# Loading keys and receptances eight tokens to a partition in a linear-attention and hypermixer kernel

## The chip, the cores and the metric

The kernel runs on one core of one Trainium2 chip. The metric is the device time of one execution in microseconds. Before the change it is 106.31 us, the median of three runs (105.37 to 106.67).

## The reference

Four batches, eight heads, 768 tokens, 48 values per head. For each head a 48 x 48 state runs over the tokens:

```
cur   = (u * k_t) outer v_t
y_t   = r_t @ (state + cur)
state = w_t[:, None] * state + k_t outer v_t
```

The rows y of all heads, 384 wide, are x of the second part:

```
W_tok = (x @ w_q) @ (x @ w_k)^T / 8          (768 x 768 in each batch)
out   = relu(W_tok @ x) @ w_out
```

All inputs and the output are float32. W_tok is not built: the kernel forms T = (x w_k)^T x, which is 64 x 384, and multiplies by x w_q.

## The kernel before, in words

**Units.** The work is cut into 12 units of 256 tokens (3 to a batch), each of two chunks of 128 tokens. For a unit W, K, R and V are loaded from DRAM. `load` (L291) puts the tokens 2p and 2p+1 of the unit into partition p, so a load is one transfer of 384 KB with 128 x 8 pieces of 384 bytes. Each of the four tensors has a ring of four buffers. V of the last batch is loaded in another way: `WHOLE = (3,)`, `load_whole` (L296), four transfers for the whole batch in 192-byte pieces that are already in the token order which the chunks need.

**A unit's steps**, by the keys that the plan gives them: `ln` (ScalarE, log of the decay, L453), `k16` and `r16` (casts to bf16, L463, mostly GpSimd), `cw` (16 matmuls of the log decay with the mask CM: a running sum over the tokens of a chunk), `ep` and `en` (ScalarE, exp of that sum and of its negative, L491 and L496), `kT` and `rT` (8 transposes each on TensorE), `ks` (copy out of PSUM), `qT` (L522), `RT` = rT x ep (VectorE, L531), `KT` = ks x en (GpSimd or VectorE, L539), `A` (products of KT and RT, chunk by chunk), `AM` (the same under the mask US, L608), `kb` and `kd` (KT transposed back), `sn` and `SB` (the state), `yi` and `ya` (the output rows), `X` (L712), which also adds `Vd`, V times the u term (GpSimd, L588). V comes into chunk order with `v16` (cast, GpSimd, L556) and `vp` (4 matmuls with the permutation PM); `VB` copies it out of PSUM. In the last batch `VB` is one cast on GpSimd (L550).

Within a chunk, column j*64 + p stands for token 2p + j: even tokens first, then odd ones. The masks CM and US and the vectors gx and gv are made for that order. RT needs ep of the token before; ep is therefore written with a shift (66 columns on for j = 0, 1 on for j = 1) into blocks of 132 columns whose first is 1.

**A batch's second part**: `xt`, `XT`, `wk`, `wq`, `QK`, `T`, `TS`, then per unit `mx` (3 matmuls), `rl` (ReLU, L396 on ScalarE or L398 on VectorE), `fp` (matmuls with w_out), `os` (copy), `st` (store).

**The order** is written out by hand: every step has a rank in `RANK`, and `ALT` says which engine takes those steps that several can do. Each engine's queue is its steps sorted by rank. `Plan.order` (L80) plays the queues through with estimated durations, only to give PSUM banks and to merge the queues into one order of program text. All loads and nearly all stores are issued from SyncE in one queue, so a transfer that waits for a buffer, or a store that waits for its `os`, holds what stands behind it. `WARM` matmuls with zeros are placed among TensorE's early steps, 9 more stand at its start.

All matmuls and transposes have line 240 in the profile (the helper `mm`), all copies L384 or L390 (the helper `copy`).

Of the kernel before, what the change touches and what calls it, by code (L numbers as in the profile page):

```python
# [10 lines left out]
F32 = mybir.dt.float32  # L11
# [22 lines left out]
class Plan:  # L34
# [131 lines left out]
    0, 0, 0, 0, 0, 20, 0, 0, 21, 1, 3, 1, 0, 0, 2, 0, 0, 3, 0, 0, 6, 0, 0, 1, 1, 2, 3, 3, 2, 4, 6,  # L166
    6, 9, 3, 6, 4, 2, 5, 7, 5, 20, 10, 24, 12, 8, 10, 15, 8, 19, 11, 16, 9, 17, 11, 25, 12, 28,
    14, 30, 32, 35, 31, 18, 57, 30, 75, 38, 4, 0, 0, 5, 0, 0, 8, 0, 0, 7, 0, 0, 5, 4, 7, 14, 7, 8,
    18, 27, 9, 15, 16, 10, 6, 23, 14, 34, 17, 12, 38, 20, 41, 22, 26, 13, 33, 17, 36, 19, 42, 45,
    43, 46, 24, 64, 33, 77, 39, 9, 0, 0, 10, 0, 0, 13, 0, 0, 15, 0, 0, 13, 9, 20, 29, 15, 16, 37,  # L170
    44, 19, 25, 23, 13, 14, 47, 24, 51, 27, 20, 49, 26, 54, 29, 48, 25, 52, 27, 58, 68, 61, 65,
    35, 74, 37, 78, 40, 81, 43, 86, 44, 91, 47, 47, 0, 0, 88, 45, 97, 50, 51, 0, 0, 111, 56, 120,
    60, 54, 0, 0, 12, 0, 0, 11, 0, 0, 17, 0, 0, 16, 0, 0, 18, 11, 16, 40, 23, 22, 39, 56, 21, 31,
    30, 15, 17, 55, 29, 63, 34, 22, 60, 32, 67, 36, 53, 28, 66, 34, 71, 38, 70, 72, 73, 80, 41,
    89, 46, 101, 55, 14, 0, 0, 18, 0, 0, 21, 0, 0, 24, 0, 0, 21, 18, 35, 50, 28, 26, 59, 76, 31,
    40, 39, 33, 24, 84, 43, 82, 42, 28, 98, 53, 83, 44, 69, 36, 90, 47, 95, 52, 103, 104, 106,
    105, 57, 119, 63, 136, 68, 22, 0, 0, 19, 0, 0, 23, 0, 0, 27, 0, 0, 37, 19, 23, 79, 42, 41, 62,
    85, 32, 45, 46, 26, 27, 94, 49, 96, 51, 30, 102, 56, 93, 50, 92, 49, 100, 54, 108, 113, 115,
    112, 61, 129, 66, 139, 71, 145, 75, 153, 77, 160, 81, 50, 0, 0, 162, 82, 189, 97, 53, 0, 0,
    173, 88, 190, 98, 52, 0, 0, 26, 0, 0, 25, 0, 0, 30, 0, 0, 32, 0, 0, 48, 25, 31, 99, 53, 52,  # L180
    87, 110, 48, 60, 59, 32, 33, 116, 58, 122, 63, 40, 117, 62, 121, 64, 114, 57, 124, 65, 128,
    68, 132, 135, 133, 134, 72, 141, 74, 172, 87, 28, 0, 0, 29, 0, 0, 36, 0, 0, 33, 0, 0, 51, 29,
    37, 107, 54, 55, 109, 126, 58, 67, 69, 36, 35, 123, 62, 138, 69, 42, 137, 73, 144, 76, 125,
    66, 131, 71, 147, 77, 149, 150, 152, 151, 79, 164, 85, 180, 91, 35, 0, 0, 31, 0, 0, 37, 0, 0,
    34, 0, 0, 61, 34, 38, 127, 65, 64, 118, 130, 59, 70, 75, 41, 39, 143, 73, 140, 70, 47, 157,
    82, 146, 78, 142, 72, 155, 81, 166, 168, 169, 170, 88, 177, 92, 192, 101, 203, 103, 212, 105,
    218, 113, 55, 0, 0, 214, 106, 227, 111, 56, 0, 0, 222, 109, 230, 113, 57, 0, 0, 39, 0, 0, 41,
    0, 0, 38, 0, 0, 45, 0, 0, 46, 0, 0, 67, 43, 44, 148, 78, 76, 154, 158, 80, 84, 85, 48, 51,
    167, 84, 52, 176, 91, 165, 87, 163, 83, 175, 90, 179, 92, 182, 185, 184, 183, 95, 200, 102,
    211, 109, 42, 0, 0, 43, 0, 0, 40, 0, 0, 74, 46, 45, 156, 80, 79, 159, 161, 83, 86, 89, 49, 53,  # L190
    171, 86, 55, 191, 100, 181, 94, 178, 93, 187, 96, 194, 101, 197, 202, 198, 199, 104, 210, 104,
    215, 110, 48, 0, 0, 44, 0, 0, 49, 0, 0, 90, 50, 54, 186, 93, 94, 95, 96, 174, 188, 89, 99, 97,
    56, 98, 58, 57, 193, 100, 59, 60, 196, 102, 206, 105, 195, 99, 201, 103, 205, 208, 204, 207,
    209, 213, 106, 216, 108, 219, 221, 108, 112, 107, 217, 107, 220, 223, 111, 110, 224, 226, 225,
    114, 228, 115, 117, 231, 233, 114, 118, 58, 0, 0, 61, 0, 0, 229, 112, 116, 234, 235, 116, 117,
    59, 0, 0, 60, 0, 0, 232, 115, 118, 236, 237, 119, 119, 120, 62, 0, 0, 1, 2, 4, 5, 7, 8, 10,
    11, 12, 13, 21, 22,
]
ALT = "DDDPDAAAAAAPPDDAADAAPAAPAAADADAAAAAAPPDPAADADPAADADADAPPAPADDAAAAAAAAAPPDPAAADAPPDPAADAAPPAPAAAAAAADAAAAPPDPAAADPPDPADADPPAPPAADADADADDDAAADAAADDA"

WARM = 12
# [3 lines left out]
def kernel(  # L205
# [27 lines left out]
    WHOLE = (3,)  # L233
# [18 lines left out]
    EW = 132  # L252
# [33 lines left out]
    pos1 = const([C, 1], I32, "pos1")  # L286
# [9 lines left out]
    def load_whole(b, q, tl):  # L296
        n_ = H // 2 * NCH
        for j in range(2):
            nc.sync.dma_start(
                out=view(tl, q * n_ * D, [[D, n_], [1, D]], p0=64 * j, pn=64),  # L300
                in_=dataclasses.replace(v, offset=(b * H * S + j) * D + q * n_ * C * D,
                                        ap=[[D2, 64], [C * D, n_], [1, D]]))

    def setup():
# [9 lines left out]
        for j in range(2):  # L314
            nc.gpsimd.iota(pos0[ds(64 * j, 64), :], pattern=[[0, 1]], base=j,
                           channel_multiplier=2)
            nc.gpsimd.iota(pos1[ds(64 * j, 64), :], pattern=[[0, 1]], base=j + 1,
                           channel_multiplier=2)
        nc.scalar.activation(gx, pos0, ACT.Exp, bias=0.0, scale=MU)
        nc.scalar.activation(gv, pos1, ACT.Exp, bias=0.0, scale=-MU)  # L320
        nc.vector.memset(CM, 1.0)
        for c in range(2):
            for j in range(2):
                m = view(CM, j * C, [[64, 2], [1, 64]], p0=c * 64, pn=64)
                nc.gpsimd.affine_select(m, m, pattern=[[1, 2], [2, 64]], compare_op=ALU.is_ge,
                                        fill=0.0, base=-j, channel_multiplier=-2)
        nc.vector.memset(ID16, 0.0)
        nc.gpsimd.affine_select(ID16, ID16, pattern=[[1, C]], compare_op=ALU.not_equal, fill=1.0,
# [5 lines left out]
        nc.vector.memset(US, 1.0)  # L334
        for j in range(2):
            m = view(US, 0, [[64, 2], [1, 64]], p0=j * 64, pn=64)
            nc.gpsimd.affine_select(m, m, pattern=[[1, 2], [2, 64]], compare_op=ALU.is_gt,
                                    fill=0.0, base=-j, channel_multiplier=-2)
# [4 lines left out]
        nc.vector.tensor_scalar_mul(US, US, gv)  # L343
# [5 lines left out]
    def permute():  # L349
        for c in range(2):  # L350
            for j in range(2):
                m = PM[ds(c * 64, 64), ds(j * C + j * 64, 64)]
                nc.gpsimd.affine_select(m, m, pattern=[[1, 64]], compare_op=ALU.not_equal,
                                        fill=1.0, base=0, channel_multiplier=-1)
# [74 lines left out]
    def unit(n, batch):  # L429
# [9 lines left out]
        for name, ap in (("wg", w), ("kg", k), ("rg", r)) + (() if whole else (("vg", v),)):  # L439
            g[name] = ring(name)  # L440
            g[name + "L"] = plan.dma((name, n), 570, 1190 + 250 * (n == 0 and name == 'kg') + 250 * (n > 2),
                                     lambda e, ap=ap, x=g[name].tile: load(b, i, x, ap),
                                     buf=g[name])[1]
# [12 lines left out]
        ln = add(("ln", n), {"A": 846}, f_ln, [g["wgL"]], lw, [g["wg"]])  # L456

        def cast16(name, src, engs):
            o = ring(name)

            def f(e):
                op = dict(A=nc.scalar.copy, D=nc.vector.tensor_copy, P=nc.gpsimd.tensor_copy)[e]
                op(view(o.tile, 0, [[64, H], [512, 2], [1, D]]),  # L463
                   view(g[src].tile, 0, [[D2, H], [D, 2], [1, D]]))
            return o, add((name, n), engs, f, [g[src + "L"]], o, [g[src]])
# [21 lines left out]
        for cs in fine:  # L487
            w_ = 512 * len(cs)

            def f_ep(e, cs=cs, w_=w_):  # L490
                nc.scalar.activation(  # L491
                    view(ep.tile, cs[0] * NP * EW + 66, [[EW, NP * len(cs)], [-65, 2], [1, 64]]),
                    at(cw)[:, ds(cs[0] * 512, w_)], ACT.Exp, bias=0.0, scale=1.0)

            def f_en(e, cs=cs, w_=w_):
                nc.scalar.activation(en.tile[:, ds(cs[0] * 512, w_)],  # L496
                                     at(cw)[:, ds(cs[0] * 512, w_)], ACT.Exp, bias=0.0,
                                     scale=-1.0)
            x = add(("ep", n, cs[0]), {"A": 190 + int(w_ * 0.837)}, f_ep, [cws], ep, [cw])
            y = add(("en", n, cs[0]), {"A": 172 + int(w_ * 0.835)}, f_en, [cws], en, [cw])  # L500
# [3 lines left out]
        def transposed(name, src, step):  # L504
            x = bank()

            def f(e):
                o = at(x, BF16)
                for hp in range(NP):
                    for j in range(2):  # L510
                        mm(view(o, hp * C + j * 64, [[512, 2], [1, 64]]),
                           src.tile[:, ds(j * 512 + hp * 128, 128)], ID16, trans=True)
# [14 lines left out]
        for cs in fine:  # L527
            n4 = NP * len(cs)

            def f_RT(e, cs=cs, n4=n4):  # L530
                nc.vector.tensor_tensor(  # L531
                    view(RT.tile, cs[0] * 512, [[C, n4], [64, 2], [1, 64]]),
                    view(at(rT, BF16), cs[0] * 512, [[C, n4], [64, 2], [1, 64]]),
                    view(ep.tile, cs[0] * NP * EW, [[EW, n4], [66, 2], [1, 64]]), ALU.mult)

# [346 lines left out]
```

## Time and profile before

| | |
|---|---|
| median of three runs | 106.31 us |
| the profiled execution | 106.1 us |
| its span | 104.4 us |
| TensorE busy | 93.2 us (89%), 1651 matmuls |
| VectorE busy | 84.4 us (81%) |
| ScalarE busy | 80.6 us (77%) |
| GpSimd busy | 69.3 us (66%) |
| moved by DMA | 24.65 MB, 236 GB/s over the span |
| chain that ended last | PE 74%, DMA 6%, POOL 5%, DVE 5% |

Read it with the queues in mind: an engine takes its instructions strictly in order, so it is not enough that an operand is there early; the instruction ahead must have gone too. The DMA line of the page counts all 16 DMA engines together: 1.0 is all sixteen at work all the time, and packets that overlap on one engine can bring it above 1. The span holds what the engines do; the time of an execution is 1.7 us longer.

### The profile page before, as it was taken

The page shows a single profiled execution, that of the slowest core. Times are in us where ns is not written, and L with a number is a line of the kernel's source. Part 1 is how long each engine was busy: PE and PEld are TensorE (multiplying, and loading weights), DVE is VectorE, ACT ScalarE, POOL GpSimd, SP SyncE. Part 2 cuts the span into 40 slices and gives each one's busy share as a digit, 9 for nine tenths or more (in the row PEclk, how much of TensorE's full clock was granted, in tenths as well). Part 3 has the DMA queues.
Part 4 walks back from the last instruction along what each step waited for, and adds up shares of the span by engine and source line. Part 5 has one row for each costly group of instructions (what it writes and reads, how often), then busy time and mean ns, then how long its engine had stood idle before and what let it go on. Part 6 is the DMA issues. An engine that isn't in the chain of part 4 may idle for free.

```text
span 104.4 us, 3964 instructions
## 1 busy us (share of the span) xinstructions
PE 93.2 (89%) x1651; PEld 69.4 (66%) x1652; DVE 84.4 (81%) x140; ACT 80.6 (77%) x122; POOL 69.3 (66%) x80
## 2 busy tenths in 40 slices
PE   5999899766998999999999899999999998999910
PEld 2356488544777786767886776887888596866500
DVE  6669996995789979979999889999899699695320
ACT  6348988759879869999999886899897954855830
POOL 6607666979998828959995699999975973000000
PEclk9999999999589999999999999999999999999999
DMA  1999999999999988999999799999993056004791
GB/s 26 296 324 325 325 318 234 309 290 237 301 342 295 246 228 206 303 254 243 310 294 256 195 264 276 244 179 172 292 349 137 0 220 238 0 9 181 295 359 72
DMA packets 56803, 24.65 MB, mean 236 GB/s; under 512 B 54480, under 2 KB 55632, under 8 KB 56784
## 3 DMA queue, kind: packets, MB, share of 16 engines
q1 hardware_dynamic: 56224, 24.19, 84.3%
q8 instruction: 13, 0.21, 0.8%
q10 hardware_dynamic: 560, 0.20, 0.7%
q14 instruction: 6, 0.05, 0.1%
HBM read 19.66 MB, written 4.72 MB: 234 GB/s over the span
## 4 chain that ended last, share of the span: by engine, by line
PE 74%; DMA 6%; POOL 5%; DVE 5%; issue 3%; ACT 2%; SPq 1%; POOLq 0%; DVEq 0%
PE PS L240 74%; DMA vg<-in_v_dram 6%; DVE KT L539 2%; POOL KT L539 2%; POOL v L556 2%; POOL Vd L588 1%; ACT ep L491 1%; ACT MX L396 1%; DVE RT L531 1%; DVE AM L608 1%; SPq L292 1%; DVE qT L522 1%; ACT os L384 0%; DVE Z L306 0%; POOL r L463 0%
## 5 line engine op out<-in xcount | busy, mean ns | idle before, releaser
L608 DVE TENSOR_TENSOR AM<-PS,US 128x1024 bf16<-128x1024 f32 x24 | 29.3, 1219 | 3.4 <-PE PS L240 3.2
L539 POOL TENSOR_TENSOR KT<-ks,en 128x1024 bf16<-128x1024 bf16 (+1 forms) x11 | 20.5, 1864 | 3.6 <-DVE ks L390 3.4
L588 POOL TENSOR_TENSOR Vd<-VB,dd 128x768 bf16<-128x768 bf16 (+1 forms) x14 | 18.1, 1294 | 1.3 <-ACT dd L384 1.2
L712 DVE SCALAR_TENSOR_TENSOR X<-PS,gx,Vd 128x768 bf16<-128x768 f32 (+1 forms) x13 | 12.4, 952 | 2.8 <-POOL Vd L588 1.4
L240 PEld LDWEIGHTS <-KT 48*128 48x128 bf16 (+1 forms) x272 | 10.9, 97 | 5.2 <-issue 2.4
L496 ACT ACTIVATE en<-PS 128x1024 bf16<-128x1024 f32 (+1 forms) x14 | 12.6, 898 | 2.0 <-PE PS L240 2.0
L491 ACT ACTIVATE ep<-PS 128x1024 bf16<-128x1024 f32 (+1 forms) x14 | 12.7, 919 | 1.3 <-ACT XT L384 0.6
L453 ACT ACTIVATE lw<-wg 128x768 bf16<-128x768 f32 x12 | 10.2, 848 | 4.5 <-DMA wg<-in_w_dram 4.4
L240 PE MATMUL PS<-wo,MX 128*128 128x384 bf16 x72 | 13.3, 326 | 0.0
L463 POOL CAST k<-kg 128x768 bf16<-128x768 f32 x11 | 9.0, 825 | 3.3 <-DMA kg<-in_k_dram 3.3
L384 ACT COPY os<-PS 128x768 f32<-128x768 f32 (+1 forms) x13 | 8.6, 680 | 2.5 <-PE PS L240 2.2
L463 POOL CAST r<-rg 128x768 bf16<-128x768 f32 x9 | 7.5, 835 | 4.3 <-DMA rg<-in_r_dram 2.3
L556 POOL CAST v<-vg 128x768 bf16<-128x768 f32 x9 | 7.4, 825 | 3.6 <-DMA vg<-in_v_dram 3.6
L240 PE MATMUL PS<-RT,KT 48*128 48x128 bf16 x192 | 9.7, 221 | 0.0
L240 PEld LDWEIGHTS <-MX 128*128 128x128 bf16 x72 | 6.5, 98 | 4.1 <-issue 0.3
L531 DVE TENSOR_TENSOR RT<-PS,ep 128x1024 bf16<-128x1024 bf16 (+1 forms) x14 | 8.4, 607 | 0.8 <-PE PS L240 0.5
L396 ACT ACTIVATE MX<-PS 128x768 bf16<-128x768 f32 (+1 forms) x11 | 8.2, 755 | 0.7 <-PE PS L240 0.6
L522 DVE TENSOR_TENSOR qT<-PS,ks 128x1024 bf16<-128x1024 bf16 x12 | 8.2, 681 | 0.4 <-issue 0.4
L240 PE MATMUL PS<-Z 128*128 128x512 bf16 x20 | 7.4, 511 | 1.2 <-DVE uT L309 1.2
L384 ACT COPY XT<-PS 128x768 bf16<-128x768 bf16 (+1 forms) x9 | 6.9, 765 | 2.0 <-PE PS L240 2.0
L240 PE MATMUL PS<-ID,r 128*128 128x128 bf16 x96 | 7.7, 226 | 0.4 <-POOL r L463 0.3
L240 PE MATMUL PS<-VB,AM 128*128 128x48 bf16 x192 | 7.9, 184 | 0.1
(83 smaller groups left out, 201.1 us busy)
## 6 DMA issues: line engine op xcount, KB each, us to landing
wg<-in_w_dram SPq DMA_DIRECT2D x12, 384.0 KB, 5.4
kg<-in_k_dram SPq DMA_DIRECT2D x12, 384.0 KB, 5.9
rg<-in_r_dram SPq DMA_DIRECT2D x12, 384.0 KB, 5.9
vg<-in_v_dram SPq DMA_DIRECT2D x9, 384.0 KB, 5.8
out_dram<-os SPq DMA_DIRECT2D x9, 384.0 KB, 3.0
vw<-in_v_dram SPq DMA_DIRECT2D x4, 288.0 KB, 6.2
out_dram<-os SPq DMA_DIRECT2D x5, 192.0 KB, 2.7
wof<-in_moe_w_out_dram SPq DMA_DIRECT2D x1, 576.0 KB, 5.4
```

The source lines that it names most:

```text
L240: return nc.tensor.matmul(o, l, rr, start=start, stop=stop, skip_group_check=True, is_transpose=trans)
L384: nc.scalar.copy(o, i)
L453: nc.scalar.activation(view(lw.tile, 0, [[64, H], [512, 2], [1, D]]), view(g["wg"].tile, 0, [[D2, H], [D, 2], [1, D]]), ACT.Ln, bias=0.0, ...
L463: op(view(o.tile, 0, [[64, H], [512, 2], [1, D]]), view(g[src].tile, 0, [[D2, H], [D, 2], [1, D]]))
L491: nc.scalar.activation(view(ep.tile, cs[0] * NP * EW + 66, [[EW, NP * len(cs)], [-65, 2], [1, 64]]), at(cw)[:, ds(cs[0] * 512, w_)], ACT.E ...
L496: nc.scalar.activation(en.tile[:, ds(cs[0] * 512, w_)], at(cw)[:, ds(cs[0] * 512, w_)], ACT.Exp, bias=0.0, scale=-1.0)
L531: nc.vector.tensor_tensor(view(RT.tile, cs[0] * 512, [[C, n4], [64, 2], [1, 64]]), view(at(rT, BF16), cs[0] * 512, [[C, n4], [64, 2], [1, ...
L539: x.tensor_tensor(KT.tile[:, cols], ks.tile[:, cols], en.tile[:, cols], ALU.mult)
L556: v16s = add(("v16", n), {"P": 826}, lambda e: nc.gpsimd.tensor_copy(view(v16.tile, 0, [[D, H], [DM, 2], [1, D]]), view(g["vg"].tile, 0, [ ...
L588: nc.gpsimd.tensor_tensor(Vd.tile[:, cols], VB.tile[:, cols], view(dd.tile, cs[0] * H, [[1, len(cs) * H], [0, D]]), ALU.mult)
L608: AMs[c] = add(("AM", n, c), {"D": 1221}, lambda e, c=c, A=A: nc.vector.tensor_tensor(view(AM[c].tile, 0, [[C, 8], [1, C]]), view(at(A), 0 ...
L712: nc.vector.scalar_tensor_tensor(view(X.tile, (2 * i + c0) * DM, [[DM, nc_], [1, DM]]), view(at(y), 0, [[512, nc_], [1, DM]]), gx, view(Vd ...
```

## The change

Keys and receptances are loaded in a new layout. A unit's 256 tokens are 32 runs of 8 tokens; a partition holds one run of one head pair (4 pairs x 32 runs = 128 partitions), 8 x 48 floats in one piece of 1,536 bytes. Each tensor takes two transfers, one for the even and one for the odd heads (hh). W and V are loaded as before, V of the last batch too, which now goes through `v16`, `vp` and `VB` like the others.

The token order in a chunk becomes j*16 + q for token 8q + j: j = 0 to 7, 16 runs to a chunk. The masks and the vectors gx and gv follow; US is made on VectorE from a table TC of token numbers. The transposes write 8 x 16 columns instead of 2 x 64. `ep` is written straight into blocks of 144 columns from column 16 on; RT reads the 128 columns from column 0, so that most columns come from 16 columns back. Columns 1 to 15 are filled by a new step `ew` on GpSimd from the block's last 16 columns. A chunk's tokens are now 128 successive ones; the ReLU brings the columns back into natural order, and a store has two pieces of 1,536 bytes for a partition instead of one of 3,072.

```diff
-    WHOLE = (3,)
+    WHOLE = ()
-    EW = 132
+    EW = C + 16
+    def load_runs(b, i, hh, tl, ap):
+        nc.sync.dma_start(
+            out=view(tl, hh * 8 * D, [[1, 8 * D]]),
+            in_=dataclasses.replace(ap, offset=((b * H + hh) * S + i * U) * D,
+                                    ap=[[2 * S * D, NP], [8 * D, 32], [1, 8 * D]]))
...
-            g[name + "L"] = plan.dma((name, n), 570, 1190 + ...,
-                                     lambda e, ap=ap, x=g[name].tile: load(b, i, x, ap),
+            if name in ("kg", "rg"):
+                g[name + "L"] = [
+                    plan.dma((name, n, hh), 420, 530 + 60 * (n > 2),
+                             lambda e, ap=ap, x=g[name].tile, hh=hh: load_runs(b, i, hh, x, ap),
+                             buf=g[name])[1] for hh in range(2)]
...
-                op(view(o.tile, 0, [[64, H], [512, 2], [1, D]]),
-                   view(g[src].tile, 0, [[D2, H], [D, 2], [1, D]]))
+                op(view(o.tile, 0, [[64, 2], [128, 8], [1, D]]),
+                   view(g[src].tile, 0, [[8 * D, 2], [D, 8], [1, D]]))
...
-                    view(ep.tile, cs[0] * NP * EW + 66, [[EW, NP * len(cs)], [-65, 2], [1, 64]]),
+                    view(ep.tile, cs[0] * NP * EW + 16, [[EW, NP * len(cs)], [1, C]]),
...
+            def f_ew(e, cs=cs):
+                o = cs[0] * NP * EW
+                nc.gpsimd.tensor_copy(view(ep.tile, o + 1, [[EW, NP * len(cs)], [1, 15]]),
+                                      view(ep.tile, o + C, [[EW, NP * len(cs)], [1, 15]]))
+            x = add(("ew", n, cs[0]), {"P": 110 + 60 * len(cs)}, f_ew, [x], ep)
...
-                for hp in range(NP):
-                    for j in range(2):
-                        mm(view(o, hp * C + j * 64, [[512, 2], [1, 64]]),
-                           src.tile[:, ds(j * 512 + hp * 128, 128)], ID16, trans=True)
+                for j in range(8):
+                    mm(view(o, j * 16, [[C, NP], [512, 2], [1, 16]]),
+                       src.tile[:, ds(j * 128, 128)], ID16, trans=True)
...
-                    view(MX.tile, cs[0] * C, [[U, NK], [1, w_]]),
-                    view(at(mx), cs[0] * C, [[U, NK], [1, w_]])), [mxs], MX, [mx])
+                    view(MX.tile, cs[0] * C, [[U * C // w_, NK * w_ // C], [8, 16], [1, 8]]),
+                    view(at(mx), cs[0] * C, [[U * C // w_, NK * w_ // C], [1, 16], [16, 8]])),
+                              [mxs], MX, [mx])
...
-                        out=out[b, ds(ii * U, U)].rearrange("(p j) d -> p j d", j=2)[
+                        out=out[b, ds(ii * U, U)].rearrange("(c p) d -> p c d", c=2)[
```

`RANK` and `ALT` are written anew, `WARM` goes from 12 to 10. In numbers of instructions: SyncE issues 89 transfers instead of 66; GpSimd has 14 copies `ew` more and 11 receptance casts instead of 9; ScalarE has 12 copies `VB` instead of 9 and no receptance casts instead of 2; TensorE has 12 matmuls with PM more and 2 with zeros fewer.

The end of SyncE's queue in the changed program, by its row there (a row is one transfer; units count from 0):

```
59 store of unit 1        65 K, unit 11 (a half)
60 R, unit 11 (a half)    66 V, unit 10
61 W, unit 10             67 W, unit 11
62 K, unit 10 (a half)    68 store of unit 2
63 R, unit 10 (a half)    69 V, unit 11
64 store of unit 0        70 to 80 the other stores
```

On TensorE the transposes of unit 10's keys are matmuls 1,158 to 1,165 of 1,662, `cw` of unit 11 begins at 1,339, `vp` of unit 11 at 1,462. Before the change the transposes of unit 10's keys were 1,171 to 1,178 of 1,652.

## The prediction, on record before the result was known

> **What bounds the kernel now.** I read the forty-slice bands first, then the windows, then SyncE's queue in order of time, then the chain and TensorE's own last third.
>
> ```profile
> PE   5999899766998999999999899999999998999910
> DMA  1999999999999988999999799999993056004791
> q1 hardware_dynamic: 56224, 24.19, 84.3%
> ```
>
> TensorE is busy nearly throughout, and the 16 DMA engines are full for the first 31 of 40 slices. Two resources run side by side near their limits. The windows (columns: busy us of PE, PEld, DVE, ACT, POOL, then clock, DMA share, GB/s) tell where which one leads:
>
> ```profile
> 4.00:8.00 4.00, 4.00 (x37) 1.95 (x36) 2.88 (x8) 2.27 (x4) 0.84 (x4) 1.00 1.18 318
> 8.00:12.00 4.00, 3.41 (x61) 2.38 (x60) 3.74 (x7) 3.63 (x6) 3.00 (x5) 1.00 1.17 325
> 20.00:24.00 4.00, 2.40 (x60) 1.83 (x55) 4.00 (x6) 2.86 (x4) 3.01 (x3) 1.00 1.11 299
> 48.00:52.00 4.00, 3.83 (x101) 3.29 (x99) 3.94 (x7) 3.82 (x6) 3.99 (x5) 1.00 1.12 307
> ```
>
> Up to about 24 us loads lead: 318 to 325 GB/s, share above 1, and TensorE either idle or busy with zero matmuls (37 matmuls in 4 us). Later TensorE leads, with the loads just ahead of it. SyncE shows the pace of the loads (start, us, transfers):
>
> ```profile
> 0.78 0.44 SPq L292 DMA_DIRECT2D wg<-in_w_dram  x1
> 4.42 1.23 SPq L292 DMA_DIRECT2D kg<-in_k_dram  x1
> 5.69 2.34 SPq L292 DMA_DIRECT2D vg<-in_v_dram  x2
> 63.48 7.51 SPq L299 DMA_DIRECT2D vw<-in_v_dram  x4
> ```
>
> The first issue takes 0.44 us, later ones 1.1 to 1.3: the queue is full and an issue waits until a transfer's worth has drained. A load of 393,216 bytes at 322 GB/s is 1.22 us, the same number. It has 1,024 packets of 384 B, 64 an engine, so 19.1 ns each; the trace's packet records give a mean of 23.0 ns, so neighbours overlap by 3.9 ns. The whole-batch load of V has 1,536 packets of 192 B (17.2 ns in the records) in each of four transfers; 7.51 us for four is only possible if they too use all 16 engines (four would need 6.6 us for one). So transfers whose outermost count is 128 or 64 are seen on all 16 engines.
>
> ```profile
> 17.55 5.83 DMA vg<-in_v_dram
> 61.41 2.10 POOL KT L539
> 69.92 0.61 PE L240 MATMUL PS<-ID,k 128*128 128x128 bf16 x8
> 99.73 0.48 ACT os L384
> ```
>
> One load of V stands in the chain early (17.55), then almost only TensorE (74% of the span). The third line is the transpose of unit 10's keys; from it to the end (104.4) 34.5 us pass, with TensorE almost always busy.
>
> **The change, part by part.**
>
> *Keys and receptances.* Each 384 KB load becomes two of 192 KB with 128 packets of 1,536 B. 1,152 packets of that size are in the records: median 65 ns, mean 68. Less the overlap of 3.9 ns I take 61 ns; the ends are 57 (68 over the share of 1.18) and 68 (no overlap). What the trace does not show is how many engines share these packets. The destination leads with 128 partitions as before, but the source's outermost count is now 4 (pairs of heads), then 32 runs, then 384 floats. Every transfer of before leads on both sides with 48, 64 or 128, all multiples of 16, so only for those an even deal over 16 is shown. Bounds: 16 engines, 128/16 x 61 = 0.49 us a transfer; one engine, 7.8 us. Between them I take four, each with one of the source's four blocks, 32 x 61 = 1.95 us: a split that gives each engine an equal piece of both outer counts (4 and 128) can have at most four pieces, and it is the reading under which the 64- and 128-count loads above come out at 16. I also take them to be the same four each time, since nothing in the queue's rows shows a rotation.
>
> The Trainium skill speaks against this change. Its page "DMA: Bandwidth & Descriptors", section "Why a DMA increments its semaphore by 16 and not by 1", states that the slowest dimension above one of each side decides: a transfer runs on the largest number up to 16 that divides both, on the lowest-numbered engines. By it these run on the same four engines and the sum is the 160 below; with 16 it would be 105. No run here shows it.
>
> Sum for the busiest four engines, which also carry their sixteenths of all else in the one queue: 48 x 1.95 = 93.7 us; W and V, 24 x 1.22 = 29.3; weights, 24 packets of 1,536 B and 48 of 256 B an engine, 2.2; the three stores queued ahead of the last load, 16 packets of 1,536 B an engine each, 2.9. The first issue is at 0.8 and the first load is read at 4.42, so 2.4 us beyond its 1.22 are latency. The last load (V of unit 11) lands at T = 0.8 + 2.4 + 93.7 + 29.3 + 2.2 + 2.9 = 131 us. TensorE's 93 us of work hides beneath that and is no longer the bound.
>
> *The end after the last load.* The loads from row 62 of the new queue on (listed with the change) are the second half of unit 10's keys, half of its receptances, a store, half of unit 11's keys, V 10, W 11, a store, V 11. From the landing of row 62 to T pass 1.95 + 0.98 + 1.95 + 1.22 + 1.22 + 0.98 + 1.22 = 9.5 us. So unit 10's keys land at T - 9.5, are cast on GpSimd (0.83) and transposed at T - 8.7. Then the line at 69.92 above tells the rest: 34.5 us, and 23 more matmuls in the changed order at 93.2/1651 = 56 ns, 1.3. The other late loads fit in: GpSimd's queue (V 10, two Vd of 1.48, V 11, two KT of 1.16) reaches unit 11's first KT at about T + 5.5, where TensorE arrives at about T + 7. Span: 131.3 - 8.7 + 35.8 = 158.4. The profiled execution took 106.1 for a span of 104.4, 1.7 around it: **160 us**. (That execution is 0.2 below the median of 106.31.)
>
> *All V on TensorE.* Batch 3 trades four transfers (7.5 us) for three V loads (3.7, counted), 12 matmuls with PM (4 take 0.50 us: 1.5 in all) and three copies out of PSUM on ScalarE (792 ns each, 2.4). All lie under the load stream; were it gone, TensorE would pay the 1.5.
>
> *The shifted decay.* ep is written straight, and GpSimd copies 15 columns a block (14 instructions of 60 or 120 columns). Nearest rows: UB cast of 8 columns 189 ns, cast of 192 columns 336 ns; 2.6 to 4.7 us in all, I take 3.3. RT (VectorE) waits for it, and behind it in GpSimd's queue wait casts, KT and Vd. With loads this late GpSimd stands idle ahead of each cast, so zero; if that cover is gone it is the second rival.
>
> *Small edits.* Transposes write 16-column runs: the same matmul takes 226 ns into 64-column runs and 229 into straight ones, so zero; the other end, twice as long, is 24 x 0.45 = 10.8 us of TensorE. ReLU reads with a stride: lw with 48-element runs takes 848 ns, a straight copy 804; at most 5%, about 0.5 us. Stores in 1,536 B packets: 2 x 65 against a mean of 130, zero. Setup gains three tiny VectorE operations (140 ns) and a 128-column table: done before the first decay load is there at 4.42. Two zero matmuls fewer: nothing. Two receptance casts move from ScalarE to GpSimd (2 x 0.83). SyncE issues 89 transfers instead of 66; at the 0.44 to 0.57 of the unthrottled rows 39 to 51 us, under the stream. Three stores stand ahead of the last loads instead of one, and a store that waits for its os holds the loads behind it: the first needs TensorE up to matmul 874 of 1,662, whose loads are ten places and more ahead, so zero; in the spread case a part of the 1.4 us that the first store waits now for dd.
>
> **The rivals.**
>
> *The packets do spread over all engines* (a deal over 16, or other four each time). For it: all 66 transfers of before do. Against: none had so small an outer count. Stream: 29.3 + 48 x 0.49 = 52.8 us, against 45 x 1.22 + 7.5 = 62.4 now. It frees TensorE's idle time of 16 to 28 us (0.61 + 1.60 + 0.43 = 2.6) and adds 1.5 for V: 106.1 - 2.6 + 1.5 = 105 us, between 100 (the whole 5.83 wait goes) and 109 (half of the GpSimd terms show). Not slower as long as a half takes under 0.69 us, where the stream is 62.4 us again.
>
> *They spread, but RT waits for GpSimd.* The copy can stand behind a KT of 2.13 us. At 1 us in each of 12 units: 105 + 12 = 117. It decides from (108.4 - 105)/12 = 0.3 us a unit. Against: GpSimd is busy 66%, and idle half of some windows.
>
> *One engine:* 48 x 7.8 = 375 us, about 440. Against: both sides divide by four.
>
> **How the numbers follow.** Four fixed engines 0.86, spread 0.08, GpSimd wait 0.03, one engine 0.02, else 0.01. The likeliest gives 160. Low end: 57 ns a packet (87.6 instead of 93.7) and a tail that is only TensorE's work behind unit 11's KT (20.2 us in before, from 84.23): 125 + 20 + 2 = 147. High end: 68 ns (104.4) and a tail of 30, as TensorE restarts after idling: 142 + 30 + 2 = 174. That holds nearly all of the 0.86, so about 0.8. About 2% is what a measurement of this kernel can tell from no change. Slower: 0.86 + 0.03 + 0.02 and 0.01 each of the spread case and the rest, 0.93; within 2%: 0.04; faster: 0.03.
>
> **What would show it.** Right: DMA share near 0.4 to 0.5 with 16 engines counted, GB/s near 155 in the loading stretch, keys and receptances the longest waits of GpSimd's casts, TensorE idle between units from the start, the last load landing near 131, stores all at the end. Landing of a half at 8 us or more, since several wait in four rings. Wrong: GB/s above 300 and share near 1 with the loads done by 65 us (spread); RT waiting for the copies on GpSimd (second rival).

## The result, and the profile after

The changed kernel takes 174.56 us, the median of four runs (173.82 to 175.7), against 105.84 us for the kernel before in the same rounds: a ratio of 1.655 (95% interval 1.640 to 1.670). The prediction was 160 with a range of 147 to 174. The direction and the mechanism (four engines) held; the size missed by 14.6 us, and the time lies just above the range. Some executions of a kernel run slower than its others; times here are medians of all runs and ratios are of the fast ones alone, so that a ratio can differ from that of the medians. The profiled execution took 175.3 us, for a span of 173.6.

The page of the changed kernel: TensorE's busy tenths, the clock granted to it, the share of the DMA engines, and the queue that carries nearly all loads and stores.

```profile
PE   7435559953506869841992399973028799999990
PEclk9955855585555678996599659999555558999998
DMA  2662555342525766252556755245275700070275
q1 hardware_dynamic: 35664, 24.19, 45.4%
```

Before, TensorE's busy tenths and its clock were nearly all nines. Here the same bytes take 32 slices of 4.3 us instead of 31 of 2.6 us, with the 16 DMA engines together about half busy, and TensorE idles in many slices. Its clock is at half in 16 of the 40.

Stretches of the same trace in which only key and receptance transfers are in flight, and one in which W and V are too (columns as in the windows of before; the last two are DMA share and GB/s):

```profile
36.00:40.00 4.00, 1.04 (x20) 0.68 (x16) 2.02 (x3) 0.10 (x1) 2.27 (x2) 0.85 0.26 98
112.00:116.00 4.00, 2.85 (x51) 1.97 (x48) 2.19 (x5) 3.09 (x6) 1.43 (x2) 1.00 0.27 100
44.00:48.00 4.00, 1.93 (x42) 1.34 (x38) 2.65 (x3) 1.94 (x2) 0.33 (x1) 0.50 0.58 164
```

A share of 0.26 is four engines of sixteen (0.25), and 98 to 100 GB/s over four engines is one 1,536-byte packet in 61 to 63 ns on each. In the packet records four to five packets are in flight in such stretches, hardly ever fewer, until the last load. Over 46.0 us of stretches without any other packet, 2,959 packets start: 62.2 ns on each of four engines. That is the reading the prediction chose, the same four engines each time.

Waits of the changed kernel (in all, times, longest):

```profile
ACT lw L463 <- DMA wg<-in_w_dram: 50.5, 11, 11.5
POOL k L473 <- DMA kg<-in_k_dram: 34.0, 7, 8.9
POOL r L473 <- DMA rg<-in_r_dram: 21.8, 8, 6.3
DVE RT L547 <- POOL ep L513: 15.2, 3, 10.9
```

The kernel before had 4.4, 3.3 and 2.3 us in the first three. W leads although its own transfers use all engines: four of its sixteen parts come behind keys and receptances. From 40.6 to 41.4 us the records have only 384-byte packets (W's or V's), and at most 4.7 of them in flight. The fourth wait is new; the prediction had costed the copy in it at zero.

### The profile page after: what moved, and what is told of

Same layout as the page of the kernel before. It is cut to its first block, busy times and chain, and to the rows that moved or that the text cites. A ratio compares the mean times of both kernels' runs of the same rounds, so it can differ in the third digit from the quotient of the medians.

```text
span 173.6 us, 4043 instructions
## 1 busy us (share of the span) xinstructions
PE 114.2 (66%) x1662; PEld 84.8 (49%) x1662; DVE 84.5 (49%) x143; ACT 82.7 (48%) x122; POOL 74.7 (43%) x93
## 4 chain that ended last, share of the span: by engine, by line
DMA 34%; SPq 27%; PE 24%; POOL 5%; issue 3%; ACT 2%; DVE 1%; POOLq 0%; ACTq 0%; DVEq 0%
PE PS L243 24%; DMA rg<-in_r_dram 19%; SPq L304 15%; SPq L298 10%; DMA wg<-in_w_dram 10%; DMA kg<-in_k_dram 5%; SPq L841 2%; POOL Vd L604 2%; POOL KT L555 1%; POOL r L473 1%; DVE AM L624 1%; DVE X L728 1%; ACT os L388 1%; POOL k L473 0%; ACT VB L388 0%
## 5 line engine op out<-in xcount | busy, mean ns | idle before, releaser
L243 PE MATMUL PS<-ID,k 128*128 128x128 bf16 x96 | 10.5, 275 | 19.8 <-POOL k L473 17.3
L243 PE MATMUL PS<-ID,r 128*128 128x128 bf16 x96 | 10.7, 280 | 17.7 <-POOL r L473 14.0
L547 DVE TENSOR_TENSOR RT<-PS,ep 128x1024 bf16<-128x1024 bf16 (+1 forms) x14 | 8.5, 609 | 27.0 <-POOL ep L513 15.2
L243 PEld LDWEIGHTS <-k 128*128 128x128 bf16 x96 | 8.1, 125 | 22.9 <-POOL k L473 19.7
L473 POOL CAST r<-rg 128x768 bf16<-128x768 f32 x11 | 9.1, 826 | 21.8 <-DMA rg<-in_r_dram 21.8
L243 PEld LDWEIGHTS <-r 128*128 128x128 bf16 x96 | 8.3, 127 | 19.2 <-POOL r L473 15.0
L243 PEld LDWEIGHTS <-KT 48*128 48x128 bf16 (+1 forms) x272 | 13.7, 111 | 5.6 <-issue 3.0
L572 POOL CAST v<-vg 128x768 bf16<-128x768 f32 x12 | 9.9, 826 | 7.4 <-DMA vg<-in_v_dram 7.3
L243 PE MATMUL PS<-CM,lw 64*128 64x128 bf16 x192 | 10.0, 262 | 2.4 <-ACT lw L463 2.4
L388 ACT CAST VB<-PS 128x768 bf16<-128x768 f32 x12 | 9.6, 801 | 3.8 <-PE PS L243 2.1
L243 PE MATMUL PS<-UB,qT 128*128 128x2 bf16 x96 | 4.3, 166 | 9.2 <-ACT MX L400 9.2
```

The lines of the kernel that those rows point to most:

```text
L243: return nc.tensor.matmul(o, l, rr, start=start, stop=stop, skip_group_check=True, is_transpose=trans)
L388: nc.scalar.copy(o, i)
L473: op(view(o.tile, 0, [[64, 2], [128, 8], [1, D]]), view(g[src].tile, 0, [[8 * D, 2], [D, 8], [1, D]]))
```

## The experiments

### How many engines

The order of the source's dimensions was changed, and with it the outermost count.

**32 runs outermost.** The tile's rows come in another order; the transposes put that right by reading the identity with a stride.

```diff
-  ap=[[2 * S * D, NP], [8 * D, 32], [1, 8 * D]]
+  ap=[[8 * D, 32], [2 * S * D, NP], [1, 8 * D]]
-  src.tile[:, ds(j * 128, 128)], ID16, trans=True)
+  src.tile[:, ds(j * 128, 128)],
+  view(ID16, 0, [[1, NP], [64, 2], [4, 16]]), trans=True)
```

> The changed kernel with one thing undone: the DRAM side of the key and receptance transfers names the 32 runs first and the 4 head pairs second, so that its outermost count is 32 instead of 4 (bytes, packets, transfers and queues are the same; the transposes read the identity with its columns in the matching order). Theory (a transfer runs on as many engines as its outermost counts allow, here 4, and always the same four): all 16 engines, a half in 0.49 us, the load stream 53 us, time 100 to 112 us. Rival one (the 48 more issues, or the 1,536-byte packets themselves, are slow): 165 us or more. Rival two (GpSimd's copy ahead of RT is the larger part of the 69 us): 150 us or more.

Measured: 115.88 us (114.24 to 116.56, 4 runs; before 106.68). Most of the 69 us is gone, but the time is above the expected 112. The transposes were the reason, as the next run shows.

**The same, with an identity permuted once.** A tile `IDP`, made in the set-up, takes the stride out of the transposes.

> The changed kernel with the source of a key or receptance transfer led by its 32 runs instead of its 4 head pairs, as in the first experiment. The rows of a tile then come in another order, and the transposes put it right by reading an identity whose rows were permuted once in the set-up, so each reads 128 successive columns again. Theory (all that the change costs is that its transfers use four engines; what the first experiment kept above the kernel before is the strided reading of the identity, 24 groups of 8 transposes by some 0.45 us, 11 us): 105 us, between 102 and 108, and 8 transposes of keys take 0.61 us and not 1.09. Rival (the new token order has a price of its own on the path: the copies on GpSimd, V of the last batch on TensorE, narrow writes): 110 to 116 with transposes of 0.61 us.

Measured: 108.01 us (10 runs), ratio 1.0085 (1.002 to 1.015). The transposes of keys and receptances in the run before, then in this one (busy, mean ns):

```profile
L243 PE MATMUL PS<-ID,k 128*128 128x128 bf16 x96 | 13.1, 294 | 1.1 <-POOL k L473 1.0
L243 PE MATMUL PS<-ID,r 128*128 128x128 bf16 x96 | 13.1, 294 | 0.6 <-POOL ep L513 0.3 <-DVE r L473 0.2
```

```profile
L243 PE MATMUL PS<-IDP,k 128*128 128x128 bf16 x96 | 7.4, 220 | 0.2
L243 PE MATMUL PS<-IDP,r 128*128 128x128 bf16 x96 | 7.4, 220 | 1.5 <-POOL r L476 0.7 <-DVE r L476 0.7
```

26.2 us of TensorE become 14.8, and 7.9 us of the time go. The stride was an artefact of the experiment; the engines explain 66.5 us of the change's 68.7. In this run's page the DMA engines are full again, with the loads done in 27 slices:

```profile
PE   5985979975979989999999999999999999999910
DMA  1999999999998999999999999990000191004892
```

**Counts of 8 and of 2.** For 8 the two transfers of a tile are led by the eight heads (128 tokens each), for 2 by two head pairs with twice the runs; tokens land in other places.

```diff
-  offset=((b * H + hh) * S + i * U) * D, ap=[[2 * S * D, NP], [8 * D, 32], [1, 8 * D]]
+  offset=(b * H * S + i * U + hh * C) * D, ap=[[S * D, H], [8 * D, 16], [1, 8 * D]]
```

```diff
-  ap=[[2 * S * D, NP], [8 * D, 32], [1, 8 * D]]
+  ap=[[2 * S * D, 2], [8 * D, 64], [1, 8 * D]]
```

> The changed kernel, with the two transfers of a tensor cut by chunk instead of by head parity: outermost 8 heads, then 16 runs. Same bytes, packets and number of transfers; the rows land in other partitions than the later steps take them for, so the output is that of other tokens. Theory: 8 engines, 16 packets each, 48 x 16 x 62 ns = 47.6 us for keys and receptances, the last load at about 85 us, a tail of 30 to 36 after it, 115 to 123 us. Rivals: as the changed kernel, 165 us or more, or, if a count under 16 does not matter, near 105.

> As the run with 8, but outermost 2, then 64 runs (two heads only are read, so the output is of other data). Theory: 2 engines, 64 packets each, 48 x 64 x 62 ns = 190 us, the last load at about 228 us, 260 to 275 us in all. Rivals: as the changed kernel, about 174 us.

**Only keys led by 4**, receptances by 32.

> The changed kernel with the receptances alone loaded runs first (outermost 32) and the keys as in the change (outermost 4). Theory: engine time on the busiest four is 24 x 1.98 = 47.6 us for K, 24 x 0.5 = 11.9 for R, with W, V, weights, stores and latency 37.6: last load at about 97 us, 128 to 140 us in all, halfway. Rival (the wait on GpSimd's copies decides): no more than 10 us better than the changed kernel's 174.

Measured: 129.58, 264.21 and 140.84 us, one run each. The first is 6.6 above its expectation, the last 0.8. The start of the last load's last packet, from the packet records, tells the stream from what follows it; n is how many key and receptance packets the busiest engine carries:

| engines | n | last load | us |
|---|---|---|---|
| 16 (permuted identity) | 384 | 71.5 | 108.01 |
| 8 | 768 | 95.7 | 129.58 |
| 4 for keys, 16 for receptances | 960 | 105.8 | 140.84 |
| 4 (the change) | 1,536 | 138.8 | 174.56 |
| 2 | 3,072 | 228.4 | 264.21 |

From 1,536 to 3,072 packets the last load moves by 89.5 us, 58.3 ns a packet. 49.3 us + n x 58.3 ns gives 71.7, 94.1 and 105.3 for the other three, within 1.6 us of each. The line describes five single profiles; its two numbers are not the prices of anything by themselves. Counted as above, in stretches of keys and receptances alone, a packet takes 61.7 ns with two engines (131.4 us of them), 62.2 with four (46.0 us) and 62.5 with eight (7.2 us). So, with 128 partitions on the other side, the outermost count of the source sets how many engines carry a transfer, for 2, 4, 8 and (by 32) 16. The Trainium skill's page "DMA: Bandwidth & Descriptors", section "Why a DMA increments its semaphore by 16 and not by 1", states the rule for both sides, the largest number up to 16 that divides both outermost counts, and these five kernels agree with it.

**Cut by head pair.** Each transfer becomes two, of 32 partitions each and led by 32 on both sides; the tiles hold what they hold in the changed kernel.

```diff
+        for p in (2 * hh, 2 * hh + 1):
+            nc.sync.dma_start(
+                out=view(tl, 0, [[8 * D, 2], [1, 8 * D]], p0=32 * p, pn=32),
+                in_=dataclasses.replace(ap, offset=((b * H + 2 * p) * S + i * U) * D,
+                                        ap=[[8 * D, 32], [S * D, 2], [1, 8 * D]]))
```

> The changed kernel with every key and receptance transfer cut in two others, each for one head pair: both heads' runs to 32 partitions, both sides led by 32, 96 KB in 64 packets of 1,536 bytes. The tiles hold what they hold in the changed kernel, no other engine's work is touched. SyncE issues 137 transfers instead of 89. Theory (only the leading count of 4 made the transfers run on four engines): loads on all 16, 105 to 112, transposes of 0.61 us for 8; SyncE needs 137 x 0.5 = 69 us to issue, about as long as the loads take, so a little of it may show. Rival A (16 engines need 128 partitions on the other side): loads on a part of the engines, 130 or more. Rival B (issuing becomes the bound): 115 or more with DMA share under 0.8 early on.

Measured: 127.02 us, ratio 1.184 (1.168 to 1.199): 47 us better than the changed kernel, 15 above the expected 112. Its SyncE queue and two windows:

```profile
20.41 1.84 SPq L305 DMA_DIRECT2D rg<-in_r_dram  x4
42.58 4.31 SPq L305 DMA_DIRECT2D kg<-in_k_dram  x4
```

```profile
44.00:48.00 4.00, 2.70 (x56) 2.16 (x55) 3.99 (x7) 3.70 (x6) 1.56 (x2) 1.00 0.64 156
60.00:64.00 4.00, 1.89 (x35) 1.30 (x35) 2.07 (x4) 2.23 (x3) 1.80 (x3) 1.00 1.09 273
```

Where keys and receptances come alone the share is 0.64, more than 8 engines' worth, and with W and V among them 1.09. In that first window 17 packets are in flight from 44.0 to 44.6 us, about as many as 16 engines show elsewhere, and 4 down to 1 from 46.2 to 47.0: all engines are used (not rival A), but they run dry. At best an issue takes 0.46 us for 98,304 bytes, 214 GB/s, so issuing alone (rival B) keeps such stretches below the 318 to 325 GB/s of before's early windows. That others take over 1 us is not explained; the last load starts at 91.3 us, 20 later than with whole tiles. This variant was left there.

### What the rest of the change costs

**Loads alone.** The kernel before, with only its key and receptance loads in two transfers led by 32 runs (tokens land in other places).

> The kernel before with only its key and receptance loads changed: two transfers of 192 KB, led by 32 runs, in 1,536-byte packets; steps, order and V as before (the keys and receptances are those of other tokens, which changes no duration). Theory (larger packets on all 16 engines cost nothing and bring little, since TensorE leads): 103 to 106.5, DMA share lower than before's in the first 31 slices, loads done earlier by 5 us or more. Rival (23 issues more in SyncE's queue or the two transfers to a tile cost more than the packets save): 108 or more.

**The rest alone.** The changed kernel with the loads of before (likewise).

> The changed kernel with keys and receptances loaded as before the change, one transfer of 384-byte packets each (so they are those of other tokens, which changes no duration): what is left of the change is the token order, the copies on GpSimd, V of the last batch on TensorE, the stores in two pieces and the new order of the steps. Theory (only the four engines cost): 104 to 109. Rival (the rest of the change costs 5 us or more): 112 or more, with the added waits in VectorE's RT for GpSimd.

**The short copy on ScalarE**, with 16 engines and the permuted identity.

```diff
-                nc.gpsimd.tensor_copy(view(ep.tile, o + 1, [[EW, NP * len(cs)], [1, 15]]),
+                nc.scalar.copy(view(ep.tile, o + 1, [[EW, NP * len(cs)], [1, 15]]),
```

> As the run with the permuted identity, with the copy of 15 columns on ScalarE right behind ep instead of on GpSimd. Theory (with loads on all 16 engines GpSimd's queue is not late and the copy there is hidden): the same as that run within 1.5 us, 103 to 108; ScalarE gets 14 short copies, about 3 us of its 83. Rival (RT waits for GpSimd in this kernel too): 2 us or more faster than that run.

Measured against the same runs of before (106.17): loads alone 104.08, ratio 0.980 (0.975 to 0.985), the one edit that gains, by about the 2% that a measurement can tell; the rest alone 113.59, ratio 1.056 (1.049 to 1.063), so the theory of 104 to 109 fell; both, on 16 engines, 1.0085; the copy on ScalarE 110.03, ratio 1.034 (1.024 to 1.044), slower than on GpSimd and outside what either side of its expectation said. So larger packets on 16 engines are worth about 2%, and the rest of the change costs more than that. Which part of the rest (the token order, V on TensorE, the new order of steps) was not taken apart. The copy on GpSimd is not shown to be the part: moving it made the kernel slower, and RT never waits for it in the trace with the permuted identity, though it does once, for 4.0 us, in that of the rest alone. No kernel here that computes the reference beats the kernel before.

### What ties the end to the late loads

The loads explain only half of the miss: the end comes 34.8 us after the last load (138.8 to 173.6), where the prediction had 27.1. Two causes were tried on the changed kernel: the copy `ew` on GpSimd, for which RT waited 10.9 us, and TensorE's clock, which is at half from 120.7 to 144.6. The lines around that wait:

```profile
127.51 0.84 ACT L463 ACTIVATE lw<-wg 128x768 bf16<-128x768 f32 x1 [11.49 <-DMA wg<-in_w_dram]
128.95 1.02 ACT L501 ACTIVATE ep<-PS 128x1024 bf16<-128x1024 f32 x1
131.73 0.83 POOL L473 CAST r<-rg 128x768 bf16<-128x768 f32 x1 [1.24 <-DMA rg<-in_r_dram]
132.50 0.29 POOL L513 COPY ep<-ep 128x120 bf16<-128x120 bf16 x1
132.82 0.69 DVE L547 TENSOR_TENSOR RT<-PS,ep 128x1024 bf16<-128x1024 bf16 x1 [10.88 <-POOL ep L513]
```

The wait is put down to GpSimd because the copy came last. But `ep` itself was ready only at 129.97, since ScalarE's queue stood behind unit 10's logarithm and its late W: most of the 10.9 us was ScalarE's.

**The copy on ScalarE; 32 matmuls on zeros ahead of unit 9's receptance transposes; both.**

```diff
+                for _ in range(32 if name == "rT" and n == 9 else 0):
+                    mm(at(x), Z[:, ds(0, C)], Z)
```

> The changed kernel (four engines as they are) with the copy of 15 columns on ScalarE right behind ep instead of on GpSimd. Theory (the copy on GpSimd, costed at zero, stands behind a cast that waits for a late receptance load; RT of unit 9 waits 10.9 us and with it the transposes of unit 10's keys): RT of unit 9 starts when ScalarE has written ep, near 130.3 instead of 132.8 in the changed kernel, and the end comes 1 to 4 us earlier: 171 to 173.5 against 174.6. Rival (another late operand holds the same transposes, so the copy is no step of the miss): 174 to 176 with the transposes of unit 10's keys at 133 or later after the start.

> The changed kernel with 32 matmuls on zeros (128x512 each) ahead of the transposes of unit 9's receptances, in the 9 us that TensorE stands idle from 120 on. Nothing else is changed. Theory (TensorE's clock falls to half when it idles and stays there for some 24 us, up to 145; this slows what runs from unit 10's keys on): granted clock 1.00 in the windows from 124 to 144, and 2 to 5 us earlier: 169.5 to 172.5 against 174.6. Rival (the last third is bound by VectorE, ScalarE and GpSimd after the late loads, the clock is no matter): 174 to 177, with the clock up or not.

> Both edits of the two runs before on the changed kernel: the copy on ScalarE, and 32 matmuls on zeros in TensorE's idle 9 us. Theory (two separate terms of the miss): their gains add, 167 to 171. Rival (one hides the other): no better than the better of the two.

Measured: 175.81, 174.76 and 175.82 us (ratios 1.650, 1.640 and 1.653, within each other's intervals and that of the change). Both theories fell as they stood. The first edit did what it should: RT starts at 130.29, 2.5 us earlier, after a wait of 8.51 us for ScalarE. With zeros alone the clock held until 131.0 and fell again. With both, this stands at the end (TensorE's transposes of unit 10's keys and of KT, ScalarE's queue):

```profile
132.28 0.62 PE L243 MATMUL PS<-ID,k 128*128 128x128 bf16 x8
137.38 0.84 ACT L463 ACTIVATE lw<-wg 128x768 bf16<-128x768 f32 x1 [4.15 <-DMA wg<-in_w_dram]
138.13 0.15 ACT L388 COPY dd<-PS 128x16 f32<-128x16 f32 x1
138.34 1.01 PE L243 MATMUL PS<-ID,KT 128*128 128x128 bf16 x8 [3.87 <-ACT dd L388]
```

TensorE gains 1.3 us at the keys (133.57 in the changed kernel) and then waits 3.87 us for a copy of 0.15 us on ScalarE. That copy stands behind unit 11's logarithm, which waits for the last W. In the changed kernel the same transposes of KT start at 138.02. Each hold hid the next.

**The logarithms moved.** Unit 11's goes behind unit 10's `ep`; then unit 10's behind unit 9's `en` as well; then also the copy on ScalarE.

```diff
+        at_ = {s_["key"]: s_ for s_ in plan.steps}
+        for x, y in ((("ln", 11), ("ep", 10, 0)), (("ln", 10), ("en", 9, 0)), ):
+            at_[x]["rank"] = at_[y]["rank"] + 0.5
```

> The changed kernel with one step moved: on ScalarE the logarithm of unit 11's decay goes from its place ahead of unit 10's small copy dd to one behind unit 10's ep. Theory (ScalarE's queue is where the late loads hold the end: this logarithm waits for W of unit 11 until 137.1, and behind it stand dd and en, for which TensorE and GpSimd wait; so the end is tied to the landing of the last W and not to unit 10's keys): the transposes of KT that start at 138.0 in the changed kernel start at 136.5 to 137, KT of unit 10 on GpSimd 1.5 us earlier than 139.0, the end 1.5 to 4 us earlier: 170.5 to 173 against 174.6. Rival (the end is tied to the last load itself, V of unit 11 at 139, or to TensorE's work at half clock): 174 to 176.

> As the run before, and the logarithm of unit 10's decay moved in the same way, from ahead of a ReLU to behind unit 9's en, so that ReLU, ep, dd and en of the work at hand do not stand behind the wait for W of unit 10 (11.5 us, to 127.5). GpSimd's copy for RT stays behind the cast of unit 10's receptances. Theory (ScalarE's queue is one holder, GpSimd's the next): TensorE's idle stretch from 120 to 129 shrinks, RT of unit 9 still starts near 132.8, and the end is 2 to 5 us earlier than the changed kernel: 169.5 to 172.5. Rival: 174 to 176.

> Both logarithms moved, and the copy of 15 columns on ScalarE right behind ep, so that RT of unit 9 waits for neither queue. Theory (the miss at the end is queue order on ScalarE and GpSimd; with both out of the way only unit 11's W ties the end, and from cw of unit 11 to the end the kernel before needs some 25 us at full clock): RT of unit 9 before 128, cw of unit 11 at 138.5 to 143 instead of 147.6, time 165 to 170. Rival (TensorE's own work after the last load is the limit, at half clock or not): 172 or more.

Measured: 172.57 (ratio 1.627, 1.620 to 1.634, clear of the change's interval), 172.38 and 173.23 us. One step moved on ScalarE takes 2 us off; the other two edits add nothing, and the third run missed its 165 to 170. In that third trace GpSimd holds TensorE next:

```profile
131.54 0.83 POOL L473 CAST r<-rg 128x768 bf16<-128x768 f32 x1 [1.25 <-DMA rg<-in_r_dram]
132.33 1.48 POOL L604 TENSOR_TENSOR Vd<-VB,dd 128x768 bf16<-128x768 bf16 x1
133.77 2.11 POOL L555 TENSOR_TENSOR KT<-ks,en 128x1024 bf16<-128x1024 bf16 x1
135.94 1.03 PE L243 MATMUL PS<-ID,KT 128*128 128x128 bf16 x8 [2.15 <-POOL KT L555]
```

KT of unit 9 has had its operands for some 13 us; it stands behind the casts of unit 10, which wait for their loads.

**Vd and KT ahead of those casts; the same with 26 matmuls on zeros ahead of unit 10's key transposes.** The list of moves gains `(("Vd", 8, 0), ("v16", 9)), (("KT", 9, 0), ("v16", 9))`.

> The run before (both logarithms moved, the copy on ScalarE), and on GpSimd Vd of unit 8 and KT of unit 9 moved ahead of the casts of unit 10's keys and receptances, which wait for late loads. Loads and everything else as in the changed kernel. Theory (what ties the end to the late loads is queue order on three engines, each hiding the next; with KT out of GpSimd's wait TensorE's transposes of it need not stand until 135.9): they start near 134, right behind unit 10's keys at 130.4, and the end comes 1 to 3 us earlier than the 173.2 of the run before: 169.5 to 172.5; TensorE is still at half clock then, having idled. Rival (the loads themselves leave no more): 173 to 175.

> The run beside it with 26 matmuls on zeros ahead of the transposes of unit 10's keys, in the 6 us in which TensorE waits for them. Theory (the rest of the miss at the end is the half clock, which counts only when no queue holds TensorE): granted clock 1.00 from 128 to the end, transposes of unit 10's keys still near 130.4, and from there the 35.8 us that the prediction had: a span near 166, time 166.5 to 170. Rival (the clock is no matter even then): the same as the run beside it within 1 us.

Measured: 170.34 us (ratio 1.595, 1.583 to 1.606) and 170.88. The holds are worth 4.2 us in all by the medians, and 6.1 by the spans of the two profiled runs (173.6 and 167.5). With them gone (the first of the two):

```profile
129.89 1.03 PE L243 MATMUL PS<-ID,k 128*128 128x128 bf16 x8 [6.27 <-POOL k L473]
133.16 0.78 PE L243 MATMUL PS<-ID,KT 128*128 128x128 bf16 x8
```

The keys' transposes start 8.8 us ahead of the last load (138.7); the prediction had 8.7. From there to the end are 37.6 us, where it had 35.8. In the second run they start at 131.19, because its last load starts at 139.6, and 37.7 us follow. The zeros did not shorten the time. Nor did they hold the clock throughout: it is at half from 133.1 to 136.5, in the other run until 133.5. Half of each of these stretches, 1.7 and 1.8 us, is the difference from 35.8. That fits the half clock as the last term, but no run shows it by itself.

## Why the prediction was wrong in size, step by step

**What bounds the kernel**: right. **Four fixed engines**: right, by five kernels and the packet records. The forecast "slower" rested on it.

**The sum for the busiest engines, T = 131**: too low; the last load's last packet starts at 138.8. The term that was mis-sized is "48 x 1.95 = 93.7" for keys and receptances, that is the 61 ns a packet. It was the median of before, 65 ns, less an overlap; the mean in the same row was 68. Undisturbed, 61 is right (62.2 counted above, and the median is still 65). But the 5,975 packets of keys and receptances that can be told apart in the changed kernel's records, ahead of the last load, took 69.7 ns on average. What they took above 65 ns adds up to 28.0 us, 7.0 for each of the four engines. Nearly all of it (27.1) lies within 1 us behind the start of a 384-byte packet, where 3,454 of the 5,975 are, and of the 413 packets over 90 ns 410 are. So a packet of keys or receptances costs more beside W or V, which the prediction had not; why, no run shows.

With 2.3 for the first packet, 1,536 x 61.5 ns = 94.5 (61.5 being the median over windows of 1 us), 7.0 for what packets took above that and the prediction's own 34.4 for W, V, weights and stores the sum is 138.2. The same sum with two engines (3.1 for this excess) gives 228.6 against 228.4; with eight (7.6) it gives 91.5 and falls 4 short. A fixed cost of each transfer, the obvious rival, is not seen: 7 us over 75 loads are 0.09 us each, which would make a packet 4 ns dearer with eight engines (16 packets of a transfer on an engine) than with two (64), and they take 62.5 and 61.7 ns. Half of the miss in the span (7.5 of 15.2 us) lies here. The stated range covers it: its upper end had 68 ns and T = 142.

**"The other late loads fit in"**: failed, and this is what took the time out of the range, whose upper end had 30 us behind the last load where the changed kernel has 34.8. The prediction followed TensorE's queue and GpSimd's to the late loads, but not ScalarE's, and on GpSimd not what stood behind the late casts. Unit 11's logarithm held dd and en (2.0 us by moving it alone), and unit 10's casts held KT (4.2 us in all with that, unit 10's logarithm and the copy out of the way too).

**"So zero" for the copy on GpSimd**: right in its effect when the copy alone is moved (175.81), and wrong in its reason. GpSimd was idle, but idle in wait for a load, with the copy behind it. That cost RT 2.5 of the 10.9 us; the rest was ScalarE's, and ScalarE held the later work too.

**The tail of 35.8 us**: right as TensorE's work; some 1.8 us of half clock fit the rest. The prediction had "TensorE restarts after idling" only in its upper end. In the spans of the profiled runs the miss of 15.2 us closes: without the holds unit 10's keys are transposed at 129.9 and not at 122.6 (7.3), the tail from there is 1.8 longer, and the holds are the other 6.1. By the medians the holds are 4.2; the 1.9 between the two is within the scatter of the runs.

**Small edits**: the narrow writes cost nothing (220 ns against 219 and 226 before). **The spread case** would have been 105 (100 to 109): with 16 engines it is 108.0.

## What to carry to other kernels

Before a transfer is reshaped for larger packets, look at the outermost count of both sides: here 4 in place of 32 cost 66.5 us, and no row of the old trace could show it, because every count in it was a multiple of 16. When loads become the bound, follow every engine's queue, not only the critical one, from each late operand to what stands behind it; an idle engine is no cover if it idles in its queue's order. And where removing a wait gives nothing, look in that run's own trace for the next hold before the theory is dropped: here three holds in two queues, ScalarE's and GpSimd's, kept the same work.

## What the runs showed of the hardware beside this

- A transpose that reads its 128x128 identity with a stride of four elements took 294 ns on average, against 220 with successive columns: 26.2 against 14.8 us for 192.
- After idling from 119.9 to 129.1, TensorE stayed at half clock for 23.9 us, though it was busy 3.49 of 4 us soon after:

```profile
124.00:128.00 4.00, 0.00 (x0) 0.00 (x0) 0.00 (x0) 0.49 (x1) 0.00 (x0) 0.50 0.48 169
132.00:136.00 4.00, 3.49 (x50) 2.50 (x48) 2.85 (x4) 1.03 (x2) 4.00 (x4) 0.50 0.72 206
140.00:144.00 4.00, 4.00 (x45) 3.65 (x44) 2.92 (x5) 2.09 (x3) 4.00 (x5) 0.50 0.02 4
144.00:148.00 4.00, 4.00 (x74) 3.03 (x74) 2.63 (x5) 3.23 (x6) 0.52 (x2) 0.93 0.00 0
```

The clock's changes in this trace lie 3.41 us or a multiple of it apart. The Trainium skill's page "TensorE: Matmul & The Clock Gate", Part 1, states that a window of about 3.4 us of sustained work releases the clock. Counted back from the change at 144.6 in steps of 3.41 us, the last step agrees, busy throughout, and the two before it, busy for 3.00 and 2.69 us, left the clock at half. How much idling a step may hold stays open: steps busy for 3.21 and 3.22 us were followed by the full clock in the two runs without holds, and one of 3.24 us was not in the run with 32 matmuls on zeros alone.
